# Pooling with the token weights as the loaded operand, the division behind it, and a written order of single steps up to unit 19

## The chip, the cores and the metric

The kernel runs on one core of a Trainium2 chip. The metric is device time in microseconds: the median of several executions of the same program, lower is better. Engines are named as in the profile: PE is TensorE's matmuls and PEld its weight loads, DVE is VectorE, ACT is ScalarE, POOL is GpSimd, and SP is the engine that issues most transfers.

## The reference

Eight batches, 576 tokens, eight heads of 64, 32 packed tokens, then a feed-forward layer from 512 over 2048 to 512, all in float32 (w_in and w_out arrive as float64):

```python
def sm_attn(qq, kk, vv):
    s = scale * np.matmul(qq, kk.transpose(0, 1, 3, 2))
    s = s - np.max(s, axis=-1, keepdims=True)
    a = np.exp(s)
    a = a / (np.sum(a, axis=-1, keepdims=True) + 1e-09)
    return np.matmul(a, vv)
p_packed = sm_attn(p, k, v)            # first softmax, over 576 tokens
out = sm_attn(q, p_packed, p_packed)   # second softmax, over 32 packed tokens
...
h = x @ w_in                           # x: out with the heads side by side
sp = np.maximum(h, 0.0) + np.log1p(np.exp(-np.abs(h)))
g = h * erf(sp)
return (g @ w_out).astype(np.float32)
```

## The kernel before

**Attention of a batch** is a generator, `attention(b)`, whose `yield`s cut it into steps. The scores `s1` of the packed tokens (4 head pairs c × 32 packed tokens on the partitions, r for the head of a pair, 576 tokens along the row) become `a1`: maximum, exponent with the sum `sm`, then reciprocal and a multiply of the whole of `a1` by it (L237). `a1` is turned on PE in 128-token chunks (`t1`, and the last 64 tokens into half of `p`), copied to `a1t`, and the pooled values are made by 40 matmuls (L257): the values of a chunk, 64 wide, are the loaded operand, and 32 columns of `a1t` are streamed. The result is `pt`, already turned. The second softmax works on `s2`, turned into `ta`, and ends in two float32r parts of its weights, `a2h` and `a2l`.

**The feed-forward layer** is folded into the packed tokens: `w_prime(b, j)` multiplies `pt` with a quarter of w_in into one PSUM tile (tag `ps_m`, one buffer, shared with the scores), ACT copies its high part `wph`, DVE makes the low part `wpl`. A *unit* n is (batch b, token half c, block i of 256 of the 2048 columns). `h_half(n, k)` makes half of its `h` with six matmuls, ACT copies it to `hs`; the gate is softplus and erf on ACT, in groups of up to three units because each needs a function table of its own, and a multiply on DVE; the gated values are split into `gh` and `gl` on DVE; `o_block` adds the unit with 24 matmuls (8 of plain float32 for the first four units) into four PSUM banks, and behind the last block of a segment ACT copies them out (`ob`). From unit 32 on the gate is made of tanh pieces. w_in and w_out land as raw 64-bit parts (SP's transfers `wi`, `wos`) and are turned into float32 by ACT (L92) and DVE (L96), then w_out is split by DVE (`wohl`, L127 and L128).

**Order.** Units of batches 0 and 1 come in half blocks, then batches 2 to 7. Up to unit 9 the order is written out by hand in calls such as the ones below; from unit 10 on a plan says which attention steps, loads and splits go with which unit, and `keep_order` ties PE, DVE, ACT and SP to the written order up to unit 16. What comes behind is set by the scheduler from the order of writing. An engine works strictly through its own row of instructions.

```python
begin_gates(3)
steps(second)
o_block(*units[3])
low = w_prime(1, 0)
low()
end_gates()
```

Of the kernel before, what the change touches and what calls it, by code (L numbers as in the profile page):

```python
# [25 lines left out]

@with_exitstack
def tile_pack_attention_moe(ctx: ExitStack, tc: tile.TileContext, qT, kT, v, pT, w_in, w_out, outT):
# [22 lines left out]
    ATT2 = 14  # L51

    LATER = (10, 17)
    TAGS = ("hs", "hs", "hs", "t1", "t1", "t1", "hs", "hs")
    AHEAD = 5
    STRICT = 16
    LEAD = 4
    BANKS = {3: 0, 4: 2}
    ENDS = (1, 4, 7, 10, 13, 16, 19, 22, 25, 28, 31)

# [63 lines left out]
    def split_w_out(f):  # L124
        both = opool.tile([P, 2, DM], F32R, name=f"wohl{f}", tag="wo")
        wo_hi[f], wo_lo[f] = both[:, 0, :], both[:, 1, :]
        nc.vector.tensor_copy(wo_hi[f], wo[f])  # L127
        nc.vector.tensor_tensor(wo_lo[f], wo[f], wo_hi[f], op=ALU.subtract)  # L128
# [13 lines left out]
    wp = {}  # L142

    STAGES = 12
    PACKS = 8

    def attention(b, roomy=False):

        at_o = {0: {"s1_0": 0, "s1_1": 2, "p": 0, "s2_0": 2, "s2_1": 0}, 1: {"s1_0": 0, "s1_1": 2}}.get(b, {})
# [44 lines left out]
        for c2 in range(2):  # L196
# [5 lines left out]
            if roomy:  # L202
                scores.append(banks[0])
            else:
                copy_out(a1[:, :, c2 * HT:(c2 + 1) * HT], banks, HT)
# [3 lines left out]
        parts = apool.tile([P, 2, 2], F32, name=f"parts{b}", tag="parts")  # L209
        if roomy:  # L210
            for c2 in range(2):
                for r in range(2):
                    nc.vector.tensor_reduce(parts[:, r, c2:c2 + 1], scores[c2][r][:, 0:HT], axis=AX.X, op=ALU.max)
# [3 lines left out]
        nc.vector.tensor_scalar(m[:], m[:], -SCALE, None, op0=ALU.mult)  # L217
        if roomy:
# [5 lines left out]
            yield  # L224
            nc.vector.tensor_reduce(sm[:], sums[:], axis=AX.X, op=ALU.add)
        else:
            if b == 1:
                yield
# [3 lines left out]
            if b == 1:  # L232
                yield
        nc.vector.tensor_scalar(sm[:], sm[:], 1e-9, None, op0=ALU.add)
        nc.vector.reciprocal(sm[:], sm[:])
        for r in range(2):
            nc.vector.tensor_scalar(a1[:, r, :], a1[:, r, :], sm[:, r:r + 1], None, op0=ALU.mult)  # L237
        yield
        a1t = apool.tile([P, NCH, 2, P], F32, name=f"a1t{b}", tag="big", bufs=3)
        banks = bank("t1")  # L240
        for j, r in [(j, r) for r in range(2) for j in range(NT)]:
            o = (j % 2 * 2 + r) * P
            nc.tensor.transpose(banks[0][j // 2][:, o:o + P], a1[:, r, j * P:(j + 1) * P], ident[:])  # L243
        copy_out(a1t[:, 0:NT].rearrange("p (x j) r k -> p x (j r k)", x=2), (banks[0], None) if roomy else banks, 512)
        yield
        banks = bank("p")
        po, pr = banks[0]
        for r in range(2):
            nc.tensor.transpose(pr[0:REM, r * P:(r + 1) * P], a1[:, r, NT * P:S], ident[:])
        nc.scalar.copy(a1t[0:REM, NT].rearrange("p r k -> p (r k)"), pr[0:REM, 0:2 * P])  # L250
        if b < 2:
            yield
        for j in range(NCH):
            n = min(P, S - j * P)
            for c in range(NC):
                for r in range(2):
                    nc.tensor.matmul(po[64 * r:64 * r + 64, NK * c:NK * c + NK],  # L257
                                     values[j][0:n, 64 * (2 * c + r):64 * (2 * c + r) + 64],
                                     a1t[0:n, j, r, NK * c:NK * c + NK], start=(j == 0 and c == 0), stop=(j == NCH - 1),
                                     skip_group_check=True)  # L260
        ptt = apool.tile([P, P], F32, name=f"pt{b}", tag="pt")
        (nc.scalar.copy if roomy else nc.vector.tensor_copy)(ptt[:], po[:, 0:P])
        pt[b] = ptt
        yield
        nb = HT // NK
        ta = apool.tile([P, 2, S], F32, name=f"ta{b}", tag="big", bufs=3)
        for c2 in range(2):
            banks = bank(f"s2_{c2}")
            for c in range(NC):
                for r in range(2):  # L270
                    nc.tensor.matmul(banks[0][r][NK * c:NK * c + NK, 0:HT], ptt[64 * r:64 * r + 64, NK * c:NK * c + NK],  # L271
                                     q[c][64 * r:64 * r + 64, c2 * HT:(c2 + 1) * HT], start=True, stop=True)
            if roomy:
# [9 lines left out]
        mx = apool.tile([P, 2, 2 * nb], F32, name=f"mx{b}", tag="mx")  # L283

        class Tokens:

            def __init__(self, h0, h1):
                self.cols = slice(h0, h1)
                self.blocks = ta[:, :, h0:h1].rearrange("p r (n k) -> p r n k", k=NK)
                self.mx = mx[:, :, h0 // NK:h1 // NK]  # L290
                self.wide = self.mx.unsqueeze(3).to_broadcast([P, 2, (h1 - h0) // NK, NK])

            def max(self):
                nc.vector.tensor_reduce(self.mx, self.blocks, axis=AX.X, op=ALU.max)

            def exp(self):
                nc.vector.tensor_tensor(self.blocks, self.blocks, self.wide, op=ALU.subtract)
                nc.scalar.activation(ta[:, :, self.cols], ta[:, :, self.cols], AF.Exp, scale=SCALE)

            def sum(self):  # L300
                self.total()
                self.share()

            def total(self):
                nc.vector.tensor_reduce(self.mx, self.blocks, axis=AX.X, op=ALU.add)

            def share(self):
                nc.vector.tensor_scalar(self.mx, self.mx, 1e-9, None, op0=ALU.add)
                nc.vector.reciprocal(self.mx, self.mx)
                nc.vector.tensor_tensor(self.blocks, self.blocks, self.wide, op=ALU.mult)  # L310

            def turn(self):
                if self.cols.stop - self.cols.start == S:
                    nc.vector.transpose(tb[:].rearrange("p r s -> p (r s)"), ta[:].rearrange("p r s -> p (r s)"))
                    return
                for r in range(2):
                    nc.vector.transpose(tb[:, r, self.cols], ta[:, r, self.cols])

            def high(self):
                nc.scalar.copy(hi[:, :, self.cols], tb[:, :, self.cols])  # L320

            def low(self):
                nc.vector.tensor_tensor(lo[:, :, self.cols], tb[:, :, self.cols], hi[:, :, self.cols], op=ALU.subtract)  # L323

        if not roomy:
            every = Tokens(0, S)
            every.max()
            every.exp()
            yield
            every.sum()  # L330
            every.turn()
            if b == 1:
                nc.vector.tensor_copy(hi[:], tb[:])
            else:
                every.high()
            every.low()
            yield
            return
        yield
        near, far = Tokens(0, HT), Tokens(HT, S)  # L340
        for c2, half in enumerate((near, far)):
            for r in range(2):
                nc.vector.transpose(ta[:, r, half.cols], scores[2 + c2][r][:, 0:HT])
            if half is near:
                near.max()
                near.exp()
        yield
        near.sum()
        near.turn()
        near.high()  # L350
        yield
        near.low()
        yield
        far.max()
        far.exp()
# [61 lines left out]
    def take(later, n):  # L417
        for step in later[:n]:
            step()
# [380 lines left out]
```

## Time and profile before

| | |
|---|---|
| median of 3 runs | 758.65 us (758.23 to 759.93) |
| the profiled execution | 756.69 us, of which 754.9 us from the first to the last instruction |
| mean granted clock of PE | 0.995 |
| PE busy | 729.1 us, 97% |
| ACT busy | 571.0 us, 76% |
| DVE busy | 549.8 us, 73% |
| POOL busy | 37.6 us, 5% |
| read from memory, written | 45.61 MB, 11.80 MB |

The busy times are those of one execution. A busy PE isn't a PE at its peak, since matmuls overlap; what a matmul costs is read from the starts of those that follow each other. A float32 matmul appears as two records. Idle time of another engine costs only where PE waits for it.

### The profile page before, as it was taken

The page shows a single profiled execution, that of the slowest core. Times are in us where ns is not written, and L with a number is a line of the kernel's source. Part 1 is how long each engine was busy: PE and PEld are TensorE (multiplying, and loading weights), DVE is VectorE, ACT ScalarE, POOL GpSimd, SP SyncE. Part 2 cuts the span into 40 slices and gives each one's busy share as a digit, 9 for nine tenths or more (in the row PEclk, how much of TensorE's full clock was granted, in tenths as well). Part 3 has the DMA queues.
Part 4 walks back from the last instruction along what each step waited for, and adds up shares of the span by engine and source line. Part 5 has one row for each costly group of instructions (what it writes and reads, how often), then busy time and mean ns, then how long its engine had stood idle before and what let it go on. Part 6 is the DMA issues. An engine that isn't in the chain of part 4 may idle for free.

```text
span 754.9 us, 15373 instructions
## 1 busy us (share of the span) xinstructions
PE 729.1 (97%) x6376; PEld 664.2 (88%) x6376; DVE 549.8 (73%) x838; ACT 571.0 (76%) x962; POOL 37.6 (5%) x56
## 2 busy tenths in 40 slices
PE   6789989999999999999999999999999999999998
PEld 5576777898889998999889989899989998999998
DVE  4868988433757697777976788776987679766664
ACT  3696897674867788786878869787787868878784
POOL 2111022011111000000000000000000000000000
PEclk9999999999999999999999999999999999999999
DMA  8956360104423310024100330022100210000000
GB/s 304 387 195 215 125 210 33 58 33 110 92 33 78 88 60 32 2 86 138 34 1 12 99 116 33 2 82 80 61 33 1 82 49 33 2 1 32 1 33 33
DMA packets 30279, 58.42 MB, mean 77 GB/s; under 512 B 3584, under 2 KB 12800, under 8 KB 30208
## 3 DMA queue, kind: packets, MB, share of 16 engines
q1 hardware_dynamic: 27136, 52.70, 20.8%
q0 software_dynamic: 3072, 4.72, 3.5%
q8 instruction: 50, 0.82, 0.4%
q14 instruction: 21, 0.17, 0.1%
HBM read 45.61 MB, written 11.80 MB: 76 GB/s over the span
## 4 chain that ended last, share of the span: by engine, by line
PE 89%; DVE 5%; ACT 4%; issue 1%; DMA 1%; POOL 1%; ACTq 0%; DVEq 0%; POOLq 0%
PE o L496 51%; PE h L441 26%; PE wp L373 4%; PE p L257 3%; PE s L271 1%; PE s L200 1%; PE t L243 1%; DMA q<-qT 1%; PE idle L627 1%; DVE hs L401 1%; ACT L393 1%; ACT t L393 1%; POOL w_in_sb L78 0%; DVE wpl L377 0%; ACT w_in_sb L92 0%
## 5 line engine op out<-in xcount | busy, mean ns | idle before, releaser
L496 PE MATMUL o<-gh,wohl 128*128 128x288 f32 x1984 | 418.3, 297 | 4.4 <-ACT ob L510 3.4
L496 PEld LDWEIGHTS o<-gh,wohl 128*128 128x128 f32 x1984 | 324.8, 188 | 16.2 <-ACT ob L510 5.0
L496 PE MATMUL o<-gl,wohl 128*128 128x288 f32 x992 | 292.2, 295 | 0.0
L496 PEld LDWEIGHTS o<-gl,wohl 128*128 128x128 f32 x992 | 186.7, 188 | 0.9 <-issue 0.9
L441 PE MATMUL h<-a2h,wph 128*128 128x288 f32 x512 | 155.1, 303 | 2.9 <-ACT a2h L320 1.1
L441 PE MATMUL h<-a2h,wpl 128*128 128x288 f32 x512 | 152.1, 297 | 1.5 <-DVE wpl L377 1.5
L441 PE MATMUL h<-a2l,wph 128*128 128x288 f32 x512 | 151.7, 296 | 0.7 <-DVE a2l L323 0.7
L441 PEld LDWEIGHTS h<-a2h,wph 128*128 128x128 f32 x512 | 96.5, 188 | 28.8 <-ACT u L471 12.6
L475 DVE SCALAR_TENSOR_TENSOR hs<-t,hs 128x576 f32<-128x576 f32 x96 | 72.5, 755 | 60.7 <-ACT t L474 60.4
L449 ACT ACTIVATE hs<-h 128x288 f32<-128x288 f32 x192 | 76.9, 409 | 51.8 <-PE h L441 50.5
L474 ACT ACTIVATE t<-t,bias 128x576 f32<-128x576 f32 x96 | 74.1, 772 | 39.9 <-DVE t L473 39.8
L441 PEld LDWEIGHTS h<-a2h,wpl 128*128 128x128 f32 x512 | 96.3, 188 | 4.6 <-issue 2.7
L441 PEld LDWEIGHTS h<-a2l,wph 128*128 128x128 f32 x512 | 96.4, 188 | 2.3 <-DVE a2l L323 1.4
L386 DVE TENSOR_TENSOR gl<-hs,gh 128x576 fp32r<-128x576 f32 x124 | 93.5, 754 | 2.1
L472 DVE SCALAR_TENSOR_TENSOR t<-t,hs 128x576 f32<-128x576 f32 x96 | 72.0, 750 | 22.9 <-ACT u L471 22.9
L385 DVE CAST gh<-hs 128x576 fp32r<-128x576 f32 x124 | 56.6, 457 | 41.8 <-PE o L496 40.0
L469 ACT ACTIVATE t<-hs,bias 128x576 f32<-128x576 f32 x96 | 74.7, 778 | 2.2
L471 ACT ACTIVATE u<-t,bias 128x576 f32<-128x576 f32 x96 | 74.4, 775 | 1.8
L470 ACT ACTIVATE t<-t,bias 128x576 f32<-128x576 f32 x96 | 74.4, 775 | 1.8
L473 DVE SCALAR_TENSOR_TENSOR t<-u,t 128x576 f32<-128x576 f32 x96 | 72.3, 754 | 1.3
L377 DVE TENSOR_TENSOR wpl<-wp,wph 128x1024 fp32r<-128x1024 f32 x32 | 38.9, 1214 | 9.5 <-ACT wph L375 9.4
L447 ACT COPY hs<-h 128x288 f32<-128x288 f32 x64 | 23.8, 403 | 25.0 <-PE h L441 24.9
(78 smaller groups left out, 615.8 us busy)
## 6 DMA issues: line engine op xcount, KB each, us to landing
k<-kT SPq DMA_DIRECT2D x32, 288.0 KB, 4.3
q<-qT SPq DMA_DIRECT2D x32, 288.0 KB, 4.4
wi<-w_in SPq DMA_DIRECT2D x16, 512.0 KB, 7.2
v<-v SPq DMA_DIRECT2D x32, 256.0 KB, 3.7
wos<-w_out SPq DMA_DIRECT2D x16, 512.0 KB, 7.5
outT<-ob SPq DMA_DIRECT2D x48, 144.0 KB, 1.8
outT<-ob POOLq DMA_DIRECT2D x32, 144.0 KB, 3.3
v<-v SPq DMA_DIRECT2D x8, 128.0 KB, 4.6
```

What stands on the lines that cost most here:

```text
L385: nc.vector.tensor_copy(ghi[:], hs[:])
L386: nc.vector.tensor_tensor(glo[:], hs[:], ghi[:], op=ALU.subtract)
L441: nc.tensor.matmul(ps[:, 0:HT], w[:, r, fo:fo + P], a[:, r, c * HT:(c + 1) * HT], start=(m == 0), stop=(m == 5))
L449: nc.scalar.mul(hs[:, k, :], ps[:, 0:HT], 0.5)
L469: nc.scalar.activation(t[:], hs[:], AF.Tanh, bias=bias[:, 0:1], scale=2.0 * T_SCALE)
L470: nc.scalar.activation(t[:], t[:], AF.Square, bias=bias[:, 1:2], scale=Q_SCALE)
L471: nc.scalar.activation(u[:], t[:], AF.Tanh, bias=bias[:, 2:3], scale=U_SCALE)
L472: nc.vector.scalar_tensor_tensor(t[:], t[:], 0.5 * A2, hs[:], op0=ALU.mult, op1=ALU.add)
L473: nc.vector.scalar_tensor_tensor(t[:], u[:], 0.5 * A1, t[:], op0=ALU.mult, op1=ALU.add)
L474: nc.scalar.activation(t[:], t[:], AF.Tanh, bias=bias[:, 3:4], scale=2.0 * A_SCALE)
L475: nc.vector.scalar_tensor_tensor(hs[:], t[:], 1.0, hs[:], op0=ALU.add, op1=ALU.mult)
L496: nc.tensor.matmul(acc[b, c][d][:, 0:HT], w[f][:, d * P:(d + 1) * P], gg[:, k, :], start=(first and k == 0 and n == 0), stop=(last and k = ...
```

## The change

**The pooling is turned around.** 32 columns of `a1t` are now the loaded operand and 64 columns of the values are streamed, so the result has the packed tokens on the partitions, r side by side along the row. The unscaled exponents are pooled; the sum's reciprocal is applied behind, in one multiply of 128×128 (`pn`, on DVE), which PE turns back with one more transpose, and ACT copies it to `pt`. The two multiplies of the whole `a1` are gone. For batch 0 both head rows are turned and pooled one behind the other.

**The order is a table up to unit 19.** Each word is one step: A, B, C a step of the attention of batch 0, 1, 2; N and X one of the second softmax of batch 0's near and far half; F a load, L and K its conversion on ACT and DVE; W, H (or G on DVE), V the three steps of `w_prime`; h, c (or d on DVE) the matmuls and the copy of half an `h` unit; s, e, m softplus, erf and gate; S (or R on ACT) and T the split of w_out; u (or U on ACT) and v the split of a gated unit; o one of four parts of a unit's `o`, p its copy out; i matmuls that only keep PE busy. `keep_order` now holds from the first to the last word. From unit 20 on the plan works as before, without the loads and splits, all of which are in the table.

```diff
+BEGINNING = """
+A A F0.2 F0.3 A F0.1 F0.0 i6 A A i9 A F3 F1.2 B F1.0 A A A F1.1 A F1.3 A A L0.2 K0.2 F2 A A A A A A A L0.1 L0.0 A F1
...
+"""
...
+    def attention(b):
+
+        fine, roomy = b < NB0, b == 0
...
+        def pool(r, po):
+
+            for j in range(NCH):
+                n = min(P, S - j * P)
+                for c in range(NC):
+                    nc.tensor.matmul(po[NK * c:NK * c + NK, 64 * r:64 * r + 64],
+                                     a1t[0:n, r, j, NK * c:NK * c + NK],
+                                     values[j][0:n, 64 * (2 * c + r):64 * (2 * c + r) + 64],
+                                     start=(r == 0 and j == 0), stop=(r == 1 and j == NCH - 1),
+                                     skip_group_check=True)
+
...
         nc.vector.tensor_scalar(sm[:], sm[:], 1e-9, None, op0=ALU.add)
         nc.vector.reciprocal(sm[:], sm[:])
-        for r in range(2):
-            nc.vector.tensor_scalar(a1[:, r, :], a1[:, r, :], sm[:, r:r + 1], None, op0=ALU.mult)
-        yield
...
-        for j in range(NCH):
-            n = min(P, S - j * P)
-            for c in range(NC):
-                for r in range(2):
-                    nc.tensor.matmul(po[64 * r:64 * r + 64, NK * c:NK * c + NK],
-                                     values[j][0:n, 64 * (2 * c + r):64 * (2 * c + r) + 64],
-                                     a1t[0:n, j, r, NK * c:NK * c + NK], start=(j == 0 and c == 0), stop=(j == NCH - 1),
-                                     skip_group_check=True)
...
+        pn = a1[:, 0, 0:P]
+        nc.vector.tensor_tensor(pn.rearrange("p (r d) -> p r d", r=2), po[:, 0:P].rearrange("p (r d) -> p r d", r=2),
+                                sm[:].unsqueeze(2).to_broadcast([P, 2, 64]), op=ALU.mult)
+        yield
+        nc.tensor.transpose(pr[:, 2 * P:3 * P], pn, ident[:])
+        if fine:
+            yield
         ptt = apool.tile([P, P], F32, name=f"pt{b}", tag="pt")
-        (nc.scalar.copy if roomy else nc.vector.tensor_copy)(ptt[:], po[:, 0:P])
+        nc.scalar.copy(ptt[:], pr[:, 2 * P:3 * P])
...
+    for word in BEGINNING.split():
+        parts[word[0]](*(int(x) for x in word[1:].split(".") if x))
+    end = len(traced)
...
+    behind = BEHIND
+    for n in range(BEGUN, len(units) + LAG):
...
     keep_order(start, end)
```

Three places of the rows that the engines work through. First PE, the pooling of batch 3 before (`p_3` is its result, `v0_3` the first 128 tokens of the values):

```order
L257 MATMUL p_3_2785<-a1t3_2774,v0_3_2486 64x32 x8
L257 MATMUL p_3_2785<-a1t3_2774,v1_3_2487 64x32 x8
L257 MATMUL p_3_2785<-a1t3_2774,v2_3_2488 64x32 x8
L257 MATMUL p_3_2785<-a1t3_2774,v3_3_2489 64x32 x8
L257 MATMUL p_3_2785<-a1t3_2774,v4_3_2490 64x32 x8
```

And now, the rows of r = 0; five alike follow for r = 1:

```order
L277 MATMUL p_3_2788<-v0_3_2494,a1t3_2707 32x64 x4
L277 MATMUL p_3_2788<-v1_3_2495,a1t3_2707 32x64 x4
L277 MATMUL p_3_2788<-v2_3_2496,a1t3_2707 32x64 x4
L277 MATMUL p_3_2788<-v3_3_2497,a1t3_2707 32x64 x4
L277 MATMUL p_3_2788<-v4_3_2498,a1t3_2707 32x64 x4
```

There are 40 matmuls in both, of 64 weights by 32 columns before and 32 by 64 now; behind the second ten rows come 17 `o` and 5 `h` matmuls and then the transpose of `pn`.

Second DVE, between the exponent's input for the near half of batch 0's second softmax and the low part of the first `w_prime`, before:

```order
L297 TENSOR_TENSOR ta0_314<-ta0_314,mx0_338 128x2x288
L343 STREAM_TRANSPOSE ta0_314<-s2_1_0_0_325 128x288
L343 STREAM_TRANSPOSE ta0_314<-s2_1_0_1_326 128x288
L305 TENSOR_REDUCE mx0_338<-ta0_314 128x2x9
L308 TENSOR_SCALAR mx0_338<-mx0_338 128x2x9
L309 RECIPROCAL mx0_338<-mx0_338 128x2x9
L310 TENSOR_TENSOR ta0_314<-ta0_314,mx0_338 128x2x288
L317 STREAM_TRANSPOSE tb0_335<-ta0_314 128x288 x2
L377 TENSOR_TENSOR wpl0_0_347<-wp0_0_348,wph0_0_346 128x1024
L323 TENSOR_TENSOR a2l0_337<-tb0_335,a2h0_336 128x2x288
```

Now, from the same instruction on (`wi0_1` is the raw part of w_in's first column block, rows 128 to 255):

```order
L178 TENSOR_TENSOR ta0_272<-ta0_272,mx0_302 128x2x288
L112 SCALAR_TENSOR_TENSOR w_in_sb_81<-wi0_1_128,w_in_sb_81 128x512
L174 STREAM_TRANSPOSE ta0_272<-s2_1_0_0_285 128x288
L174 STREAM_TRANSPOSE ta0_272<-s2_1_0_1_286 128x288
L182 TENSOR_REDUCE mx0_302<-ta0_272 128x2x9
L112 SCALAR_TENSOR_TENSOR w_in_sb_81<-wi0_3_118,w_in_sb_81 128x512
L184 TENSOR_SCALAR mx0_302<-mx0_302 128x2x9
L185 RECIPROCAL mx0_302<-mx0_302 128x2x9
L112 SCALAR_TENSOR_TENSOR w_in_sb_81<-wi0_0_130,w_in_sb_81 128x512
L187 TENSOR_TENSOR ta0_272<-ta0_272,mx0_302 128x2x288
L193 STREAM_TRANSPOSE tb0_299<-ta0_272 128x288 x2
L176 TENSOR_REDUCE mx0_302<-ta0_272 128x2x9
```

Three conversions of w_in have moved in between, and the maximum of the far half; a conversion of `wi1_2`, `a2l0` and `wpl0_0` follow.

Third ACT, ahead of the high part of `w_prime(1, 2)`, before (`t1_0_3` is the gate of batch 1, half 0, block 3):

```order
L393 ACT_TABLE_LOAD
L393 ACTIVATE t1_0_3_1168<-hs1_0_3_1038 128x576
L393 ACTIVATE t1_1_0_1170<-hs1_1_0_1103 128x576
L393 ACTIVATE t1_1_1_1172<-hs1_1_1_1151 128x576
L399 ACT_TABLE_LOAD
L399 ACTIVATE t1_0_3_1168<-t1_0_3_1168 128x576
L399 ACTIVATE t1_1_0_1170<-t1_1_0_1170 128x576
L399 ACTIVATE t1_1_1_1172<-t1_1_1_1172 128x576
L92 CAST wo10_1180<-wos10_995 128x512
L375 CAST wph1_2_1221<-wp1_2_1223 128x1024
```

And now:

```order
L436 ACTIVATE t1_0_3_1144<-hs1_0_3_1024 128x576
L429 COPY hs1_1_1_1132<-h1_1_1_1_1159 128x288
L143 CAST wohl8_1169<-wo8_1006 128x512
L481 COPY ob0_1_3_3_1212<-o0_1_0_3_822 128x288
L436 ACTIVATE t1_1_1_1222<-hs1_1_1_1132 128x576
L439 ACT_TABLE_LOAD
L439 ACTIVATE t1_1_1_1222<-t1_1_1_1222 128x576
L439 ACTIVATE t1_0_3_1144<-t1_0_3_1144 128x576
L108 CAST wo10_1235<-wos10_1167 128x512
L395 CAST wph1_2_1264<-wp1_2_1246 128x1024
L439 ACTIVATE t1_1_0_1141<-t1_1_0_1141 128x576
```

The group of three gates is taken apart: copies and a split stand between its steps, and the third erf has moved behind the high part.

More of the change, by code (lines that the diff above doesn't have):

```diff
@@ L282, in attention @@
         a2[b] = (hi, lo)
[L283 to L336, printed above, removed]
+        mx = apool.tile([P, 2, S // NK], F32, name=f"mx{b}", tag="mx")
+        if roomy:
+            halves["N"] = second_softmax(b, ta, tb, mx, hi, lo, 0, HT, scores[2])
+            halves["X"] = second_softmax(b, ta, tb, mx, hi, lo, HT, S, scores[3], nc.vector.tensor_copy)
@@ L337, in attention @@
             yield
             return
[L339 to L354, printed above, removed]
@@ L355, in attention @@
[L355 to L364 removed]
+        every = second_softmax(b, ta, tb, mx, hi, lo, 0, S, None, nc.vector.tensor_copy if fine else nc.scalar.copy)
+        for k, _ in enumerate(every):
+            if fine or k in (2, 8):
+                yield
     def w_prime(b, j):
[L368 removed]
@@ L408, in tile_pack_attention_moe, with w_prime_high @@
-    unsplit = []
-    def split_for(n):
-        while unsplit and unsplit[0][1:] in [u[:3] for u in units[n:n + 2]]:
-            split_g(*unsplit.pop(0))
-    held = []
-    rows = {}
-    def take(later, n):
-        for step in later[:n]:
-            step()
-        del later[:n]
-    def h_half(n, k, later=None):
+        raw[b, j] = ps
+    def w_prime_high(b, j, copy=nc.scalar.copy):
+        hi = wpool.tile([P, 2, FB], F32R, name=f"wph{b}_{j}", tag="wph")
+        copy(hi[:], raw[b, j][:])
+        wp[b, j] = (hi, wpool.tile([P, 2, FB], F32R, name=f"wpl{b}_{j}", tag="wpl"))
@@ L458, in h_block, with split_for @@
+    def split_for(n):
+        while unsplit and unsplit[0] in (n, n + 1):
+            split_high(unsplit[0])
+            split_low(unsplit.pop(0))
     def h_block(n):
-        h_half(n, 0)
-        h_half(n, 1)
+        for k in range(2):
+            h_half(n, k)
+            h_copy(n, k)
         if n < GROUPED:
-            if n in ENDS and n >= ALONE:
-                begin_gates()
-                end_gates()
+            group.append(n)
+            if n in ENDS:
+                for part in (softplus, erf, gate):
+                    for m in group:
+                        part(m)
+                unsplit.extend(group)
+                group.clear()
```

490 lines of the change are left out of this document (214 added, 276 removed).

## The prediction

> **What bounds the kernel now.** I read the page first, then busy time by stretches, PE's list of waits, and the chain of waits in time order. Of the page:
>
> ```profile
> span 754.9 us, 15373 instructions
> PE 729.1 (97%) x6376; PEld 664.2 (88%) x6376; DVE 549.8 (73%) x838; ACT 571.0 (76%) x962; POOL 37.6 (5%) x56
> ```
>
> PE is busy 97% of the span, the next engine 76%. The stretches (length, PE busy, PE loads, DVE, ACT, POOL, PE clock, DMA share, GB/s) say where PE isn't:
>
> ```profile
> 0.00:30.00 30.00, 20.00 (x263) 15.62 (x264) 17.67 (x37) 12.95 (x27) 4.17 (x8) 0.94 0.95 340
> 30.00:145.00 115.00, 105.05 (x841) 86.56 (x840) 88.65 (x141) 89.96 (x151) 16.80 (x28) 0.99 0.46 159
> 70.00:90.00 20.00, 16.87 (x131) 13.65 (x131) 19.44 (x29) 16.42 (x28) 2.50 (x4) 1.00 0.29 87
> 110.00:120.00 10.00, 6.91 (x49) 5.02 (x49) 8.85 (x15) 3.81 (x9) 2.69 (x4) 0.83 0.08 29
> 145.00:200.00 55.00, 52.20 (x456) 48.25 (x455) 24.99 (x43) 36.28 (x62) 6.79 (x9) 1.00 0.31 78
> 200.00:700.00 500.00, 500.00 (x4435) 462.15 (x4434) 385.23 (x571) 395.09 (x663) 9.80 (x11) 1.00 0.17 49
> ```
>
> From 200 to 700 us PE is never idle, so there only less PE work brings anything. PE idles 10.0 us between 30 and 145 us (two of the worst stretches stand below that row) and 2.8 us from there to 200 us; before 30 us stands the start. The waits of PE from 28 to 180 us:
>
> ```profile
> PE o L496 <- ACT ob L510: 3.4, 2, 2.0
> PE wp L373 <- DVE wpl L377: 3.1, 1, 3.1
> PE h L441 <- DVE wpl L377: 1.5, 2, 0.7
> PE o L496 <- ACT hs L447: 1.2, 1, 1.2
> PE s L271 <- DMA q<-qT: 0.8, 2, 0.4
> ```
>
> No resource carries these: each is one step standing behind others in a queue. So the change has two accounts: PE work of the six batches behind the beginning (2 to 7), and waits in the first 145 us.
>
> **The pooling, batches 2 to 7.** Rows of the chain of waits (start, length, what) show two neighbouring `o` units, the first and last of five such rows of pooling (batches 3 to 7), and eight fp32 `o` records; two rows of PE in order of time show a `wp` block and what follows it; the last is a group by line:
>
> ```profile
> 442.93 3.18 PE o L496 x24
> 447.69 3.19 PE o L496 x24
> 254.52 2.57 PE p L257 x80
> ...
> 607.76 2.57 PE p L257 x80
> 50.58 1.94 PE o L496 x8
> 105.00 1.09 PE L373 MATMUL wp<-w_in_sb,pt 64*32 64x512 f32 x16
> 106.02 0.40 PE L441 MATMUL h<-a2h,wph 128*128 128x288 f32 x1
> L257 PE MATMUL p<-a1t,v 128*64 128x32 f32 x512 | 17.2, 227 | 0.0
> ```
>
> A unit (12 `h` and 24 `o` matmuls) takes 447.69 − 442.93 = 4.76 us, and pooling holds PE for 2.57 us in every later batch: 40 matmuls in 80 records. An fp32 record streams at 1.94/8 = 0.243 us for 288 columns, 0.84 ns a column, so 32 columns are 27 ns. The weights are 64 wide and r alternates, so two records can run side by side: 40 pairs of 64 ns, 27 of them streaming. The other 37 ns is what each 128 columns of weights cost beside it. The change makes 20 groups of four (column strips c = 0..3), with 4 × 32 = 128 columns of weights and a stream of 64 columns, 54 ns. Bounds:
>
> - Low: four run together and the stream or the weights hide the other: 20 × 64 = 1.3 us.
> - Weights and stream one after the other: 20 × (37 + 54) = 1.8 us.
> - Not more than two together: 40 × (54 + 37/2) = 2.9 us.
> - High: no overlap of strips at all: 80 × 54 = 4.3 us.
>
> The nearest row for 32-wide strips is `wp`: 16 records of 512 columns would stream 16 × 432 ns = 6.9 us one by one and took 106.02 − 105.00 = 1.02 us. Strips thus run beside each other nearly seven deep, and I take 1.6 us, between the first two. The new PE transpose of `pn` is one record of 128 columns, 0.84 × 128 = 108 ns, 0.11 us. In the order a stretch of `o` and `h` lies between pooling, that transpose and the `s2` behind it, which covers DVE's multiply and ACT's copy. Per batch 1.6 + 0.11 − 2.57 = −0.86 us; six batches −5.2 us (−7.0 by the low bound, +2.6 by two together, +11 by no overlap).
>
> The Trainium skill's TensorEngine Tiling (Array Packing), Performance Considerations, recommends just this swap where the moving side is 32 wide, with four column strips. Its TensorE: Matmul & The Clock Gate, Part 3, speaks against: weight loads overlap running matmuls only if the row group differs, and here all strips use all 128 rows. By that rule, with its P/1.2 per load, a group would be an estimated 4 × 27 + 54 = 161 ns, 3.2 us in all. For the pair of before the same rule gives 2 × 53 + 27 = 133 ns, where the rows show 64, so the measurement decides against it.
>
> **What goes with it.** Two scalings of `a1` on DVE (L237) leave each batch and a multiply of 128×128 comes; one 128×128 copy goes from DVE to ACT. At 385 and 395 of 500 us busy both have cover from 200 us on; without it a batch's extra ACT copy would cost under 0.4 us. I count nothing. Batch 2's wait for q goes or stays by SP's order:
>
> ```profile
> 172.85 6.52 DMA q<-qT
> ```
>
> Three of its four q loads are issued only after the pooling; the new order issues all four behind v, in a row, and the swap frees v earlier. Between 0 and its 0.8 us I take −0.7.
>
> **The beginning, start.** Rows of PE, ACT and DVE in order of time from the first softmax to `wpl0_1` (start, length, engine, line):
>
> ```profile
> 13.02 0.16 DVE L225 TENSOR_REDUCE sm<-sums 128x2 f32<-128x4 f32 x1 [1.55 <-ACT a L222]
> 13.61 0.95 DVE L237 TENSOR_SCALAR a<-a,sm 128x576 f32<-128x576 f32 x2
> 17.01 3.35 PE L257 MATMUL p<-a1t,v 128*64 128x32 f32 x80
> 20.40 0.27 ACT L262 COPY pt<-p 128x128 f32<-128x128 f32 x1 [1.62 <-PE p L257]
> 21.55 0.85 DVE L343 STREAM_TRANSPOSE ta<-s 128x288 f32<-128x288 f32 x2 [2.05 <-PE s L271]
> 28.69 0.74 DVE L323 TENSOR_TENSOR a2l<-tb,a2h 128x576 fp32r<-128x576 f32 x1
> 29.35 1.89 DVE L96 SCALAR_TENSOR_TENSOR w_in_sb<-wi,w_in_sb 128x512 uint32<-128x512 uint32 x3
> 31.15 0.75 DVE L294 TENSOR_REDUCE mx<-ta 128x18 f32<-128x576 f32 x1
> 35.49 1.23 DVE L377 TENSOR_TENSOR wpl<-wp,wph 128x1024 fp32r<-128x1024 f32 x1
> ```
>
> The sum and division leave the path (13.02 to 14.56, 1.5 us), r = 0 turns and pools while r = 1 is still in the exponent, and pooling shrinks. I expect `pt` about 3.3 us earlier, so DVE's transposes at about 18.2. But ahead of `wpl0_0` DVE now carries three w_in conversions that were done before 21.55 and one of the next block, 4 × 1.89/3 = 2.5 us, and the far half's maximum, 0.75: its end is 18.2 + (29.43 − 21.55) + 3.25 = 29.3, against 29.43. Behind it DVE does the same work as before plus an `h` copy and the high half of `wp0_1`, about 1.5 us more, up to the end of `wpl0_1` (36.72 now). The gain at `pt` is thus spent on DVE: between −2 and +2, I take +0.5. The `h0_0_0` half behind `wp0_1` covers 0.8 of its wait.
>
> **The beginning, 37 to 145 us.** The largest loss, with its queue, in rows of ACT and DVE in order of time and of the chain of waits (the last of them a steady `h` unit):
>
> ```profile
> 103.63 1.83 ACT L393 ACTIVATE t<-hs 128x576 f32<-128x576 f32 x3
> 105.48 1.28 ACT L399 ACT_TABLE_LOAD   x1
> 106.78 1.83 ACT L399 ACTIVATE t<-t 128x576 f32<-128x576 f32 x3
> 109.15 1.00 ACT L375 CAST wph<-wp 128x1024 fp32r<-128x1024 f32 x1
> 112.86 1.22 DVE L377 TENSOR_TENSOR wpl<-wp,wph 128x1024 fp32r<-128x1024 f32 x1
> 114.14 1.96 PE wp L373 x16
> 116.10 2.47 PE h L441 x12
> 451.90 1.78 PE h L441 x12
> ```
>
> `wp1_2` was done by 106; its high half stood behind a whole gate group on ACT, its low half behind three gates and a w_out split on DVE, and `wp1_3` waited 3.1 us for the one buffer. The clock row of 110–120 reads 0.83, and `wp1_3` took 1.96 instead of 1.02 us, the `h` unit behind it 2.47 instead of 1.78: the place costs about 3.1 + 0.9 + 0.7 = 4.7 us. The Trainium skill's clock-gate page (Part 1) has the same: an idle window of about 3.4 us halves the clock, and the trace agrees.
>
> In the new order one gate, not three, lies between that high half and its low half on DVE, and one erf stands behind, not ahead. ACT still has three softplus and two erf ahead of it, so I take 3.5 of the 4.7, between 0 and 4.7. Of the other idle time between 30 and 145 us (10.0 − 3.1 = 6.9 us) I take a third, −2.0 (bounds 0 and −6.9), since DVE is busy 19.44 of 20 us in 70–90 and gets thirteen `h` copies and four 1024-wide casts from ACT for eight w_out and three gate casts that go the other way, and since two more table loads of 1.28 us fall on ACT. Batch 1's pooling gives −0.86. The wait for `ob` at 150 us lies behind the table's end; I leave it. Beginning in all: +0.5 − 3.5 − 2.0 − 0.9 = −5.9, bounds −13 (all 12.8 us of idle time up to 200 gone) and +6 (new waits as long as half of the old).
>
> **Sum.** −5.2 − 0.7 − 5.9 = −11.8 us against the profiled execution's 756.69: 744.9. The median of the runs, 758.65, stands 1.96 above that execution, so the forecast for a median is 746.9, say 747.
>
> **Rivals.**
> - *The order brings nothing.* DVE and ACT, busy 89 and 90 of 115 us between 30 and 145, hand new waits back for the old. For it: DVE's 19.44 of 20 us and the start above. Then −5.2 − 0.7: 752.7.
> - *The swap is at par.* Weights and stream in series over all strips, 20 × (2 × 37 + 54) = 2.6 us a block, or two strips together, 2.9: +0.1 to +0.4 a batch; the order still gains 5.0 and the q wait 0.7: 754 to 757, say 755. Against it stands the `wp` row.
> - *No overlap of strips, slower.* Pooling at 4.3 us is +1.84 a batch, +14.7 over eight; with the order's 5.0 and the q wait 768. It decides where 8 × (x + 0.11 − 2.57) passes 5.7, at x = 3.2 us a block. The clock-gate page's rule on row groups, above, (the Trainium skill) would put the block at that point and the time at 759, no change; the 64 ns of the rows leave it 0.01 of this case's chance.
> - *The fixed order misses.* PE idles anew at `wp0_1` and behind, beyond 3 us at a time, with the half clock on top, more than 6 us net: 760.
>
> **How the numbers follow.** Forecast 0.58, order nothing 0.22, par 0.08, no overlap 0.04, order misses 0.08. Its own range is 740 to 751. The range 739 to 756 leaves out the two slower cases and the low tail. Faster by over 0.2% (1.5 us, about what a measurement tells from no change): 0.58 + 0.21 + 0.07 = 0.86; within, from the edges of the second, third and last case: 0.01 + 0.01 + 0.02 = 0.04; slower: 0.04 + 0.06 = 0.10.
>
> **What would show it.** Pooling blocks of 1.3 to 1.8 us in the chain, PE 100% busy from 200 us, a unit still 4.76 us; no 0.83 in the clock between 100 and 125 us; first `h` near 28 to 30 us; batch 3's pooling, at 254.52 now, 5.9 + 0.7 + 0.9 us earlier, near 247. I am wrong if pooling stays above 2.4 us, or PE's idle time between 30 and 145 us stays near 10 us.

## The result and the profile after

| | before | after |
|---|---|---|
| median of the runs made together, us | 758.44 (757.67 to 759.93) | 734.81 (734.51 to 735.12) |
| ratio, 95% interval | | 0.9686 (0.9669 to 0.9703) |
| span of the profiled execution, us | 754.9 | 733.3 |

The kernel is 3.1% faster, twice what I forecast and below my range. The page of the changed kernel:

```profile
span 733.3 us, 15411 instructions
PE 720.5 (98%) x6400; PEld 656.3 (89%) x6400; DVE 547.8 (75%) x831; ACT 573.0 (78%) x965; POOL 36.7 (5%) x56
```

PE's busy time falls by 8.6 us, the span by 21.6. By stretches (columns as in the prediction):

```profile
0.00:30.00 30.00, 22.34 (x281) 16.80 (x281) 18.86 (x39) 12.10 (x26) 5.23 (x10) 0.94 0.96 347
30.00:145.00 115.00, 112.97 (x937) 96.63 (x936) 95.86 (x153) 102.52 (x168) 17.14 (x30) 1.00 0.48 164
70.00:90.00 20.00, 19.92 (x163) 17.47 (x162) 19.20 (x27) 18.35 (x32) 2.21 (x5) 1.00 0.45 146
110.00:120.00 10.00, 10.00 (x77) 10.00 (x77) 7.75 (x13) 9.07 (x17) 3.25 (x6) 1.00 0.54 198
145.00:200.00 55.00, 55.00 (x514) 49.20 (x513) 32.19 (x47) 39.53 (x64) 7.16 (x8) 1.00 0.34 72
200.00:700.00 500.00, 500.00 (x4449) 463.66 (x4448) 382.61 (x566) 399.76 (x679) 7.14 (x8) 1.00 0.17 49
```

Between 30 and 145 us PE idles 2.0 us in place of 10.0, although DVE and ACT are busier there than before (95.86 and 102.52 of 115 us); 110 to 120 us has its full clock. PE's longest waits all lie in the first 38 us now:

```profile
PE idle L620 <- POOL ident masks.py:199: 4.8, 1, 4.8
PE h L421 <- DVE wpl L400: 1.5, 2, 0.7
PE p L347 <- DVE a L344: 1.3, 1, 1.3
PE h L421 <- ACT hs L429: 0.5, 1, 0.5
```

The 3.1 us for `wpl` at `wp1_3`, the 3.4 us for `ob` and the wait for `q` are gone. In the chain of waits stand the first and last of five rows of pooling (batches 3 to 7) and two neighbouring `o` units:

```profile
235.19 1.66 PE p L277 x80
...
585.85 1.66 PE p L277 x80
...
679.30 3.19 PE o L472 x24
684.07 3.19 PE o L472 x24
```

**Where the time went.** The same two blocks of work in both kernels, the second `wp` block of batch 2 and the third of batch 7, in PE's rows in order of time; before:

```profile
209.69 1.09 PE L373 MATMUL wp<-w_in_sb,pt 64*32 64x512 f32 x16
...
649.11 1.09 PE L373 MATMUL wp<-w_in_sb,pt 64*32 64x512 f32 x16
```

and after:

```profile
191.73 1.09 PE L389 MATMUL wp<-w_in_sb,pt 64*32 64x512 f32 x16
...
627.48 1.09 PE L389 MATMUL wp<-w_in_sb,pt 64*32 64x512 f32 x16
```

At batch 2 the new kernel is 17.96 us ahead, at batch 7 21.63. So five batches give (21.63 − 17.96)/5 = 0.73 us each, and 18 us come from the beginning, where I had put under 8. With the swap alone (the first experiment below) the block of batch 2 starts at 208.42 us, so the order's part, 16.7 us, is complete there.

To see where in the beginning, I price each PE record at its undisturbed cost (0.133 us an `h` or split `o` record, 0.243 a plain `o`, 1.02 a `wp` block, other blocks at theirs) and call the rest of the time lost. The third column is the first experiment below, the swap alone:

| time lost by PE, us | before | after | swap alone |
|---|---|---|---|
| 0 to 37.5 us | 23.95 | 25.32 | 25.72 |
| 37.5 to 90 | 8.52 | 1.98 | 10.02 |
| 90 to 145 | 7.35 | 1.81 | 8.54 |
| 145 to 180 | 5.15 | 1.57 | 1.74 |
| behind | 15.13 | 14.55 | 16.11 |

The new order does nothing for the start and takes some 15 us of lost time out of 37.5 to 180 us. The table uses some modelled prices, so its tenths mean little. Lost time is more than idle time: a matmul whose neighbour starts 0.13 us behind it counts as busy for 0.29 us when nothing follows.

### The profile page after: what moved, and what is told of

The parts are those of the page before. It is cut to its first block, busy times and chain, and to the rows that moved or that the text cites. A ratio compares the mean times of both kernels' runs of the same rounds, so it can differ in the third digit from the quotient of the medians.

```text
span 733.3 us, 15411 instructions
## 1 busy us (share of the span) xinstructions
PE 720.5 (98%) x6400; PEld 656.3 (89%) x6400; DVE 547.8 (75%) x831; ACT 573.0 (78%) x965; POOL 36.7 (5%) x56
## 4 chain that ended last, share of the span: by engine, by line
PE 88%; DMA 4%; DVE 4%; issue 1%; ACT 1%; SPq 0%; POOL 0%; POOLq 0%
PE o L472 54%; PE h L421 26%; PE wp L389 4%; DMA wos<-w_out 1%; PE p L277 1%; DMA wi<-w_in 1%; PE s L359 1%; PE s L252 1%; DMA k<-kT 1%; DMA v<-v 1%; PE t L267 1%; DVE gl L456 0%; DVE wohl L146 0%; DVE wpl L400 0%; ACT wo L108 0%
## 5 line engine op out<-in xcount | busy, mean ns | idle before, releaser
L472 PE MATMUL o<-gh,wohl 128*128 128x288 f32 x1984 | 422.7, 298 | 0.0
L389 PE MATMUL wp<-w_in_sb,pt 64*32 64x512 f32 x512 | 37.1, 601 | 0.2 <-DVE w_in_sb L112 0.2
```

Of the source, the lines that this page charges most:

```text
L389: nc.tensor.matmul(ps[NK * c:NK * c + NK, r, :], pt[b][64 * r:64 * r + 64, NK * c:NK * c + NK], w_in_sb[64 * r:64 * r + 64, c, j * FB:(j + ...
L472: nc.tensor.matmul(acc[b, c, d][:, 0:HT], w[f][:, d * P:(d + 1) * P], gg[:, k, :], start=(first and k == 0 and m == 0), stop=(last and k = ...
```

## The experiments

The runs were made on several occasions, and the median of the kernel before was 757.6 to 758.4 us on them. A difference of about 1 us between two kernels of different occasions means nothing.

**The two parts apart.** First the kernel before with only the pooling turned around:

```diff
-                    nc.tensor.matmul(po[64 * r:64 * r + 64, NK * c:NK * c + NK],
-                                     values[j]..., a1t[0:n, j, r, ...], ...)
+                    nc.tensor.matmul(po[NK * c:NK * c + NK, 64 * r:64 * r + 64],
+                                     a1t[0:n, j, r, ...], values[j]..., ...)
```

> The kernel before with the pooling turned around and the division behind it, in the old hand-written order (from batch 2 on with the extra step). Theory A (the swap is worth its PE time, eight times 2.57 - 1.66 less the transpose, and the rest came from the order): 758.4 - 6 = 752, pooling blocks of 1.66 us, the waits in 30 to 200 us as before. Rival B (the earlier packed tokens also shorten the waits of the beginning): 748 or less.

Measured: 751.58 us (750.05 to 752.02), ratio 0.9901 (0.9865 to 0.9938): 6.8 us, where theory A had some 6. Second the new order with the old pooling:

> The changed kernel with the 40 pooling matmuls in the old orientation (values loaded, 32 columns streamed, both head rows behind one another); the multiply and the transpose behind stay, so the packed tokens come out wrongly scaled and turned. Theory A: 734.8 + 8 x 0.91 = 742, PE's idle time in 30 to 145 us stays near 2 us. Rival B: 746 or more, with new waits in the beginning.

Measured: 742.51 us (740.68 to 742.62), ratio 0.9786 (0.9745 to 0.9827). So the order is worth 15.9 us on the old pooling and 751.58 − 734.81 = 16.8 on the new, the swap 6.8 and 7.7: the parts add up within the noise, and the order is the larger one. (The kernel with the order alone still carries the new multiply and transpose, so its two figures aren't quite the order and the swap.) Busy time from 30 to 145 us, swap alone:

```profile
30.00:145.00 115.00, 103.34 (x823) 84.93 (x823) 87.20 (x138) 88.96 (x149) 16.84 (x28) 0.97 0.45 155
```

and order alone:

```profile
30.00:145.00 115.00, 113.05 (x933) 97.32 (x933) 95.74 (x152) 102.02 (x168) 17.19 (x30) 1.00 0.48 163
```

The waits go with the order; the swap alone leaves them.

**What makes the pooling block short.** The changed kernel with its pooling loops exchanged, so that neighbours in PE's row share a column strip:

```diff
-            for j in range(NCH):
-                n = min(P, S - j * P)
-                for c in range(NC):
+            for c in range(NC):
+                for j in range(NCH):
+                    n = min(P, S - j * P)
```

> The changed kernel, with the pooling's loops exchanged: all five chunks of one column strip (c), then the next strip, and not the four strips of one chunk. The same 40 matmuls, the same sums. Theory A (the pooling block takes 1.66 us because four neighbours in the row lie in four column strips and run beside each other; five neighbours in one strip can't): a block of 3 to 4.3 us (80 records of 54 ns is 4.3), so 745 to 756 us. Rival B (the overlap needs no neighbours in other strips, a 32-wide load is merely short): a block of 1.6 to 2.0 us and 734 to 738 us.

Measured: 771.85 us (770.59 to 772.07), ratio 1.018 (1.0154 to 1.0206). The chain of waits, batch 3:

```profile
247.37 6.32 PE p L277 x80
```

Theory A, and worse than its upper end. 8 × (6.32 − 1.66) = 37.3 us, and the time rose by 37.0. The averages, 79 ns a record in one strip and 83 ns a group of four strips, hide two things that the starts of the single records show. Within the four full chunks, records of one strip start 56 ns apart, which is the stream of 64 columns (54 ns) alone; with the four strips as neighbours, four records start 6 to 7 ns apart and the next four 56 ns after the first. So four strips share the time of one stream, and no time for weights shows in either. The rest stands where the shape changes, from chunks of 128 rows to the last one of 64 tokens and back: a step of about 150 ns to the first record behind each change, and some 25 ns more right behind it. A block of the changed kernel has four such changes, 0.54 of its 1.66 us; with the loops exchanged there are 16, 1.8 of the 6.32 us. So of the 4.66 us between them 3.4 are the strips and the others the changes of shape.

The Trainium skill's TensorE: Matmul & The Clock Gate, Part 3, says that weight loads overlap a running matmul only in another row group. By that rule, with its P/1.2 for a load (LDWEIGHTS), two records of one strip would start an estimated 27 + 54 = 81 ns apart, and a group of four would take 161. The average of 79 ns looks like it, but the single starts are 56 ns apart, and the group of four takes 56; in the full chunks all of them use all 128 rows. So the measurement decides against the rule for these matmuls.

**DVE and ACT sharing.** The changed table with all copies and splits on the engines that had them before:

```diff
-... h1.0 h1.1 c1.1 d1.0 ... G0.1 ... R1 T1 ... U7 ...
+... h1.0 h1.1 c1.1 c1.0 ... H0.1 ... S1 T1 ... u7 ...
```

> The changed kernel with the same order of steps, but every step back on its old engine: the thirteen h copies on ACT, the eight w_out and three gate casts on DVE, the four casts of w_prime on ACT. Theory A (the order brings the 15 us): 735 to 738. Rival C (the sharing out between DVE and ACT brings it): 741 to 747.

Measured: 741.2 us (740.87 to 741.27): 6.4 us more, at the lower end of rival C; theory A missed. And the other way, the same sharing in the old order:

```diff
-                nc.scalar.copy(hs[:, k, :], ps[:, 0:HT])
+                (nc.vector.tensor_copy if (n, k) in ON_DVE else nc.scalar.copy)(hs[:, k, :], ps[:, 0:HT])
...
```

> The kernel before, with the work of the beginning shared between DVE and ACT as the changed kernel shares it: the same thirteen copies of half an h unit and the same four high parts of w_prime on DVE, the same eight high parts of w_out and three of gated units on ACT. Order and pooling as before. Theory A (sharing is worth its 6 us by itself, as the changed kernel lost 6.4 us without it): 751 to 754 us against 758.4. Rival B (sharing pays only in an order that lets the other engine take the work at once; in the old order each moved step stands behind as much as it did): 757 to 762, no change or slower.

Measured: 767.72 us (765.35 to 768.46), ratio 1.0123 (1.0093 to 1.0153): slower than rival B's upper end. DVE's rows in order of time show it:

```profile
32.03 0.46 DVE L448 COPY hs<-h 128x288 f32<-128x288 f32 x1 [2.28 <-PE h L442]
33.47 0.46 DVE L448 COPY hs<-h 128x288 f32<-128x288 f32 x1 [0.98 <-PE h L442]
33.84 0.68 DVE L96 SCALAR_TENSOR_TENSOR w_in_sb<-wi,w_in_sb 128x512 uint32<-128x512 uint32 x1
```

DVE stands idle for PE's `h` while three conversions of w_in wait behind the copy; they began at 29.35 us before. A shared step pays only where the row around it is written for it.

**One step moved in the old order.** Three parts of `w_prime(1, 2)` ahead of the gate group:

```diff
+                early = [it for it in plan.get(n + 1, []) if it == ("wp", 1, 2)]
+                do(early)
```

> The kernel before with one step moved: the three parts of w_prime(1, 2) ahead of the gate group that stood in front of its high half on ACT. Theory A (that place costs 3.1 us of waiting and about 1.6 of half clock): 758.4 - 4.7 = 753.7, no 0.83 in the clock of 110 to 120 us. Rival D (DVE is the bound there, and the wait turns up at the next step): 757 to 758.5.

Measured: 760.48 us (757.69 to 763.24), ratio 1.0028 (1.0006 to 1.005). The 4.7 us did not come; PE's row shows why:

```profile
106.17 1.96 PE L373 MATMUL wp<-w_in_sb,pt 64*32 64x512 f32 x16 [3.00 <-DVE wpl L377]
```

`wp1_2` itself now waits 3.0 us for the one buffer, and behind that it takes 1.96 us instead of 1.09. **The same place in the new order,** with W1.2, H1.2 and V1.2 directly ahead of W1.3:

```diff
-... W1.2 v10 o10.2 K10 H1.2 S10 h14.1 V1.2 ... K12 R12 T12 W1.3
+... v10 o10.2 K10 S10 h14.1 ... K12 R12 T12 W1.2 H1.2 V1.2 W1.3
```

> The changed kernel, with the three steps of w_prime(1, 2) (W1.2, H1.2, V1.2) moved from their places spread over unit 14 to directly ahead of W1.3, which shares their one buffer. Theory A (what the new order gained at this place is the distance between the two products of weights; without it PE stands for the high part, 1.0 us, the low part, 1.2, and what is ahead of them on ACT and DVE, and the half clock follows): 737.5 to 740 us, 2.7 to 5 more than 734.8; a wait of PE for wpl of 2 to 4 us stands at W1.3. Rival B (with the gates taken apart nothing long stands ahead of the two parts, and PE's wait is only the two parts themselves, without the half clock): 736.5 to 737.5, a wait of about 2.2 us.

Measured: 742.01 us (741.29 to 743.16), 7.2 us more; both theories were too low. PE's row, DVE's rows and the window's clock:

```profile
105.54 1.09 PE L389 MATMUL wp<-w_in_sb,pt 64*32 64x512 f32 x16
111.34 1.96 PE L389 MATMUL wp<-w_in_sb,pt 64*32 64x512 f32 x16 [4.71 <-DVE wpl L400]
```

```profile
109.15 0.69 DVE L146 TENSOR_TENSOR wohl<-wo,wohl 128x512 fp32r<-128x512 f32 x1 [1.44 <-ACT wohl L143]
110.06 1.22 DVE L400 TENSOR_TENSOR wpl<-wp,wph 128x1024 fp32r<-128x1024 f32 x1 [0.22 <-ACT wph L395]
```

```profile
110.00:120.00 10.00, 8.66 (x58) 7.00 (x59) 3.29 (x5) 3.04 (x7) 1.49 (x3) 0.71 0.35 130
```

The wait is longer than the two parts (2.2 us), because the split of w_out ahead of them is itself waiting for ACT, and the clock falls to 0.71, which is 2.9 of the 10 us. The wait and the slower clock add up to 7.6 us, about the 7.2 measured.

**Batch 1's attention later.** The changed table, with the B words from the ninth on (the exponents, one step behind the maximum that the expectations name) 18 words later, 6 words later, or only the second scores and softmax 9 words later (of which this is a piece). Counted in the table as written they stand 14 to 17, 2 to 6 and 5 to 9 places further down:

```diff
-h6.0 h6.1 o0.1 o1.2 B B c6.1 o1.3 e2 m2 o1.1 c6.0 s5 B h7.0 h7.1 ...
+h6.0 h6.1 o0.1 o1.2 c6.1 o1.3 e2 m2 o1.1 c6.0 s5 B h7.0 B h7.1 ...
```

> The changed kernel, with the steps of batch 1's attention from its maximum on (word B, from the ninth on) each written 18 words later, the last of them right before the first half of unit 8. Nothing else moves, and no work changes. Theory A (the order's gain of some 16 us comes from batch 1's chain of single steps, which now starts six to seven units of time earlier and so no longer leaves PE without a unit to work on between 60 and 90 us): 738 to 741 us, 3 to 6 more than the changed kernel's 734.8, and PE busy in 70 to 90 us falls from 19.92 of 20 us to under 18. Rival B (the gain is that no step stands behind a long row of others; when batch 1's chain starts matters little, since h and o units of batch 0 are there to be done meanwhile): 734.5 to 737, PE busy in 70 to 90 us above 19.

> The changed kernel, with the steps of batch 1's attention from its maximum on each written 6 words later (not 18, which cost 21.7 us). Theory A (the time that batch 1's chain takes from the maximum to the low part of its second weights decides PE's waits up to 90 us, and the table has little slack for it): 738 to 744 us, 3 to 9 more than 734.8. Rival B (there is slack of several words, and the 21.7 us came from the last nine steps, which 18 words pressed together ahead of unit 8): 734.5 to 737 us.

> The changed kernel, with only the second scores and second softmax of batch 1 (word B from the twentieth on) each written 9 words later; the pooled tokens come as early as they do. Theory A (the second half of the chain is what PE needs on time: unit 8's first half stands right behind it): 738 to 744 us, with a wait of PE for a2h at unit 8 of 2 us or more. Rival B (PE's waits of the 18-word kernel came from the pooling, at 41 to 52 us, and its tail alone has slack): 734.5 to 737 us.

Measured: 756.48 us (754.86 to 757.35), 750.37 (749.47 to 750.61) and 747.5 (746.2 to 749.06). All are beyond theory A's upper ends, by 15.5, 6.4 and 3.5 us. The end of this chain on DVE, `a2l` of batch 1, in the kernel before (with the low part behind it):

```profile
74.70 1.36 DVE L323 TENSOR_TENSOR a2l<-tb,a2h 128x1152 fp32r<-128x1152 f32 x1
75.97 1.22 DVE L377 TENSOR_TENSOR wpl<-wp,wph 128x1024 fp32r<-128x1024 f32 x1
```

in the changed kernel:

```profile
69.31 1.36 DVE L197 TENSOR_TENSOR a2l<-tb,a2h 128x1152 fp32r<-128x1152 f32 x1
70.59 1.22 DVE L400 TENSOR_TENSOR wpl<-wp,wph 128x1024 fp32r<-128x1024 f32 x1
```

and with the second softmax 9 words, the chain 6 words and 18 words later:

```profile
80.66 1.35 DVE L197 TENSOR_TENSOR a2l<-tb,a2h 128x1152 fp32r<-128x1152 f32 x1
```

```profile
84.25 1.35 DVE L197 TENSOR_TENSOR a2l<-tb,a2h 128x1152 fp32r<-128x1152 f32 x1
```

```profile
88.48 1.36 DVE L197 TENSOR_TENSOR a2l<-tb,a2h 128x1152 fp32r<-128x1152 f32 x1
```

Against the changed kernel `a2l` comes 11.35, 14.94 and 19.17 us later, and the time is 12.7, 15.6 and 21.7 us longer: a microsecond for a microsecond and up to a tenth more. Unit 8 is the first of batch 1, and PE meets these weights with no slack. PE's rows there, in the kernel before and in the changed one:

```profile
77.25 0.40 PE L441 MATMUL h<-a2h,wpl 128*128 128x288 f32 x1 [0.73 <-DVE wpl L377]
```

```profile
71.86 0.40 PE L421 MATMUL h<-a2h,wpl 128*128 128x288 f32 x1
```

In the one the matmul waits 0.73 us for the low part, in the other it starts 0.05 us behind that part's end (70.59 + 1.22 = 71.81). With the second softmax late PE waits 4.49 us at the unit's first matmul, two matmuls sooner, and this one takes 0.61 us instead of 0.40:

```profile
80.43 0.61 PE L421 MATMUL h<-a2h,wph 128*128 128x288 f32 x1 [4.49 <-DVE a2h L195]
```

This is the cleanest of the three: up to the first `wp` block of batch 1 (66.36 us against 66.19) PE is as early as in the changed kernel. Its waits between there and unit 8 are these and 1.0 us for `a2l`:

```profile
PE h L421 <- DVE a2h L195: 4.5, 1, 4.5
PE o L472 <- ACT ob L481: 3.8, 2, 2.8
```

They come to 9.3 us, and the clock of 0.83 in 70 to 90 us takes another 3.4: together the 12.7. So the late weights cost directly, and in part through `ob`, whose copies at 69.52 us stand right behind the late exponents on ACT. Of the other two runs, in which everything from the exponents on comes later, the equal delay of `a2l` and of the end doesn't say which causes which.

A few words cost so much because a word's place holds four engines to it: with the chain 6 words later PE stood for the exponents, and every step behind followed:

```profile
42.00 1.89 PE L267 MATMUL t<-ident,a 128*128 128x128 f32 x8 [2.90 <-ACT a L316]
```

**The chain sooner in the old order** (swap alone, with batch 1's steps from the turning on one to three lines earlier):

```diff
     end_gates()
+    steps(second, 2)
     h_half(4, 0, later)
...
     h_half(5, 0)
+    steps(second)
     convert(wos[0:2])
```

> The kernel with the old, hand-written order and the swapped pooling (751.6 us), and in it only the steps of batch 1's attention from its second chunk turning on written one to three lines earlier: turned right behind the first group of gates, pooled behind h unit 5, its second scores beside the first two o units, its second softmax one unit sooner. No finer steps, no other sharing between DVE and ACT. Theory A (how early batch 1's second weights are ready sets when unit 8 can start, in the old order too; their low part ended at 78.65 us there and ends at 70.67 in the changed kernel): the low part ends 3 to 6 us sooner and the time is 746 to 749 us. Rival D (as with w_prime(1, 2) moved by itself, a chain moved without the steps around it only shifts the waits): 750 to 754 us.

Measured: 748.77 us (748.39 to 749.19), against 751.58 (750.05 to 752.02) for the swap alone. Their ratios, 0.9881 (0.9849 to 0.9913) and 0.9901 (0.9865 to 0.9938), were taken on different occasions and overlap; the ranges of the times don't. DVE's row:

```profile
73.48 1.36 DVE L329 TENSOR_TENSOR a2l<-tb,a2h 128x1152 fp32r<-128x1152 f32 x1
```

`a2l` ends at 74.84 instead of 78.65, 3.8 us sooner, and the span falls by 3.2 (750.2 to 747.0). So the chain pays by itself in the old order too, by the times though not by the ratios. The other 4.2 us to 70.67 came only with the table, and they lie behind the pooled tokens: `pt` of batch 1 comes in this kernel even sooner than in the changed one, on ACT here and there:

```profile
52.80 0.24 ACT L267 COPY pt<-p 128x128 f32<-128x128 f32 x1
```

```profile
53.66 0.25 ACT L351 COPY pt<-p 128x128 f32<-128x128 f32 x1
```

From there to the end of `a2l` it is 21.8 us here and 16.8 in the changed kernel, so an early first half of the chain alone waits in the second.

**Holding the order.** The changed kernel, its table held only up to the word h10.0:

```diff
+        if word == "h10.0":
+            end = len(traced)
```

> The changed kernel, with its order of single steps written as it is, but held on PE, DVE, ACT and SP only up to the word h10.0 (about half of the table); behind it the scheduler may put ready instructions of an engine ahead of others. Theory A (the written order itself, not its being held, brings the gain, and the scheduler follows it nearly): 733 to 737 us. Rival B (the scheduler's own choice brings back waits of PE between 80 and 200 us as the kernel before had them there, 5.6 us between 90 and 145 us and 4.0 up to 200): 739 to 745 us.

Measured: 737.56 us (736.49 to 738.47), 2.7 more and between the two theories. For the second half of the table, the order as written brings most of it; the first half stayed held.

**A better version?** Nine words of the start exchanged:

```diff
-B L1.0 X K1.0 h1.0 h1.1 c1.1 d1.0 F6 L1.1 K1.1 L1.3 K1.3 X h0.0 W0.1 ...
+L1.0 K1.0 h1.0 c1.0 L1.1 K1.1 h1.1 L1.3 K1.3 d1.1 X B F6 h0.0 W0.1 ...
```

> The changed kernel, with nine words of the start in another order: in DVE's row the maximum of batch 1's scores and the sum of the far half behind three conversions of w_in's second block, and the copy of the first half of h unit 1 on ACT (of the second half on DVE). w_prime(0, 1), which now waits for those conversions until 33.7 us, could then run at 32.4, and the h half behind its low part 0.8 to 1.3 us sooner. Theory A (what is left to gain lies in DVE's row up to 38 us, and the maximum has room, since ACT takes the exponent behind it two microseconds after its end): 733.6 to 734.4 us against 734.8. Rival B (the delay of batch 1's chain costs as much or more): 734.8 to 737.

Measured: 735.94 us (734.53 to 736.44): rival B, no gain. Nothing here beats the changed kernel.

## Why the prediction was wrong

- **The swap: the size right, its price by luck.** I took 1.6 us a block, it is 1.66. I had it between 20 times the old pair and 20 times weights and stream one after the other. The starts show no time for weights: 20 groups of 56 ns are 1.1 us, and the other 0.54 us are the changes to the last chunk's 64 rows and back, for which I had no term. The old pairs, too, start 58 to 59 ns apart and not 64, so beside their stream stand 32 ns and not the 37 that I took for weights. The transpose of `pn` costs 0.12 (a start-to-start of 0.03 and then 0.22 where 0.13 is usual), I took 0.11. A batch gains 0.73 instead of 0.86; 0.91 − 0.12 = 0.79 is explained, the other 0.06 is open. The unit stays at 4.77 us, PE at 100% from 200 us on. My parts of the swap, −5.2 − 0.7 − 0.9, make just the 6.8 us that it measured alone; to the tenth that is luck, since the interval goes from 4.7 to 10.2 us.
- **Batch 3's pooling** stands at 235.19 us, where 247 was forecast: the whole miss lies ahead of it.
- **The wait for q: right.** It is gone in the changed kernel and with the swap alone.
- **The start: right.** I put +0.5; the time lost up to 37.5 us grew by 1.4. The first `h` is at 28.08 us (28 to 30 forecast) and the second low part ends at 37.4 (36.72 before), since the gain at `pt` is spent in DVE's row, as I walked it.
- **`wp1_2` and `wp1_3`: the right mechanism, sized a little low.** I took 3.5 of 4.7. All of it went, and undoing this place costs 7.2.
- **"Of the other idle time … I take a third, −2.0": the step that failed.** It is the largest part of the miss. My beginning was −5.9, of which −0.9 is batch 1's pooling, so −5.0 for the order; the runs show −16.8. The table of lost time has 8.0 us of it (swap alone against after) in 37.5 to 90 us and 6.7 in 90 to 145, of which 4.7 are the place at `wp1_3`: this term, put at 2.0, was about 10. Two things were wrong in it.

  First its bound. I took the 12.8 us of idle time up to 200 us as all there was to win, and a third of what was left in 30 to 145 us. Of the 12.8 us 10.7 went. And idle time isn't lost time: by the prices above PE lost 18.9 us between 30 and 145 us, where the row showed 10.0 idle, and the changed kernel loses about 7 there with 2.0 idle. The slower clock is only 1.7 us of the difference (0.83 over 110 to 120 us); the rest are single matmuls that end late ahead of a wait or start about 0.24 us apart instead of 0.13 behind one, or where the kind of matmul changes, and count as busy. Much of this last part stays in the changed kernel.

  Second the cause. I read PE's waits one by one, as single steps behind others in a queue, and argued from DVE's 19.44 of 20 us that little could go. A full row doesn't show that: DVE has 19.20 of the 20 us now, and PE is busy for 19.92. What came late was a chain over several engines, batch 1's attention, whose second softmax ends on DVE at 76.06 us in the first third of that row, and which unit 8 needs. Its exponents were done at 36.9 us and turned at 49.5, with the scaling in between, behind w_out's conversions. In the old kernel this is written in these rows, of ACT, DVE and PE:

```profile
36.12 0.76 ACT L230 ACTIVATE a<-a,m 128x576 f32<-128x576 f32 x1
...
44.65 1.32 DVE L96 SCALAR_TENSOR_TENSOR wo<-wos,wo 128x512 uint32<-128x512 uint32 x2 [1.65 <-ACT wo L92]
45.89 0.16 DVE L234 TENSOR_SCALAR sm<-sm 128x2 f32<-128x2 f32 x1
46.09 0.17 DVE L235 RECIPROCAL sm<-sm 128x2 f32<-128x2 f32 x1
46.29 0.95 DVE L237 TENSOR_SCALAR a<-a,sm 128x576 f32<-128x576 f32 x2
...
49.54 0.71 PE L243 MATMUL t<-ident,a 128*128 128x128 f32 x5
```

  But the scaling isn't what held them. With the swap alone it is gone, and they are done at 39.2 us and turned at 51.84, again 12.7 us later; it is the place of the turning in PE's written row:

```profile
38.42 0.76 ACT L230 ACTIVATE a<-a,m 128x576 f32<-128x576 f32 x1
...
51.84 1.04 PE L241 MATMUL t<-ident,a 128*128 128x128 f32 x8
```

  The new order turns them at 38.88:

```profile
38.88 1.04 PE L267 MATMUL t<-ident,a 128*128 128x128 f32 x8
```

  From the swap alone to the changed kernel `a2l` comes 78.65 − 70.67 = 8.0 us sooner. At a microsecond each that would be about half of the 16.8, but this is argued: a run shows it for 3.8 of the 8.0 us alone (2.8 us of time), and the waits that PE itself has between 40 and 90 us with the swap alone are for `hs`, `ob`, `wohl`, `pt` and once for `wpl`, none for `a2l`. 4.7 us are the place at `wp1_3`; the other 4 or so are spread, and no run names them one by one.
- **"The wait for `ob` at 150 us lies behind the table's end; I leave it": wrong.** Its 2.0 us are gone. The swap alone leaves 1.2 us of them (at 155.08 us), the changed kernel none: PE is busy for 32.2 of the 35 us from 145 to 180 before, 33.8 with the swap alone and 35.0 now.
- **The rivals.** That the order brings nothing (0.22) rested on busy DVE and ACT. Both became busier (ACT with three more table loads, where I had counted two), and PE waits less: a nearly full engine need not be the bound where its row is in the sequence in which PE needs the results. Neither sign of being wrong that I named came: pooling fell to 1.66 us and the idle time to 2.0, and the forecast was wrong all the same.

The single undoings cost 6.4 (sharing), 7.2 (one place), 2.7 (holding) and 12.7 to 21.7 us (the chain), far more than 16.8 in sum. They are not shares of the gain: in a held order a late step can stop four engines and drag the others with it. Not every move does: the nine words of the last experiment cost nothing clear of noise.

## What to carry to other kernels

Before you size a gain from waits, price PE's work at its undisturbed starts and take the rest of the time as lost; here the idle time showed 10.0 of 18.9 us. Then look for the chain that ends at the next stage's first matmul, here a softmax across DVE, ACT and PE, and count how long each of its steps lay ready before it was done; an engine at 97% in that stretch is no reason to expect nothing from another order of its row. Matmuls of 32 columns of weights belong side by side in different column strips, with the strip as the innermost loop. Average over a block only after a look at its single starts: here they parted the strips from the changes of shape. Whether fewer such changes, with the last chunks of both head rows side by side, would win part of the 0.54 us a block, no run tried.

## What the hardware showed unexpectedly

The order of two loops around the same 40 matmuls changes their time from 1.66 to 6.32 us. Neighbours in four column strips start 6 to 7 ns apart, and a group of four takes 56 ns, as long as one record in one strip. At a change between 128 and 64 rows the next record starts about 150 ns behind the last one. And a wait costs more than its length: with the 4.71 us at `wp1_3` the clock is 0.71 over 110 to 120 us, and the time grew by 7.2 us.
